# A new table of thresholds for the order planner of a gated two-branch attention kernel

## The chip, the cores and the metric

The kernel runs on one core of a Trainium2 chip. Its engines are named as the profile names them: PE (TensorE, matrix products; PEld is its weight load), DVE (VectorE), ACT (ScalarE), POOL (GpSimd) and SP (SyncE, which issues the DMAs). The metric is the time of one execution on the device in microseconds. The kernel before was timed three times: 816.85, 817.59 and 822.19 us, median 817.59.

## What is computed

For 2,048 tokens of width 640 and 32 heads of width 20: branch A is full softmax attention, branch B attends to 8 positions, its own and those 2, 4 ... 14 before it, and a gate per token mixes the two.

```python
x = A_x
g = _sigmoid((x * gate_w).sum(-1, keepdims=True))
a = _A_ref(x, A_wqkv, A_wo)      # full attention
b = _B_ref(x, B_wqkv, B_wo)      # window of 8, dilation 2
return g * a + (1 - g) * b

# _A_ref
scores = jnp.einsum("bhqd,bhkd->bhqk", q, k) * scale
p = _softmax(scores, axis=-1)
o = jnp.einsum("bhqk,bhkd->bhqd", p, v)
...
# _B_ref: W, dil = 8, 2; idx = pos - off, masked where negative
logits = jnp.einsum("bhsd,bhswd->bhsw", q, kg) * scale
attn = _softmax(logits, axis=-1)
o = jnp.einsum("bhsw,bhswd->bhsd", attn, vg)
```

## The kernel before

**Blocks and tiles.** The scores of branch A are cut into blocks of 128 keys x 512 queries of one head: 32 heads x 4 query chunks x 16 key blocks = 2,048 blocks. Four heads and one query chunk make a group of 64 blocks, and there are 32 groups. `next_tile` puts two or three blocks of one group together to a tile; `qk` (L1556 to L1587) issues their score matmuls (L1569) into one of two score buffers in PSUM, and `exp` (L1589) has ACT take the exponential of the whole tile in one instruction (L1592), two-wide (128 x 1024) or three-wide (128 x 1536). The third 512 columns of a score buffer are a bank which is also lent to other work, so a tile is three-wide only when that bank is free.

**Blocks on DVE.** Where a tile is two-wide, its third bank can hold a block that "rides": `wanted` decides whether DVE takes it. DVE then computes the exponential as an integer: it adds an offset and converts to 16 bits (L1582), so that the bits read as bf16 are 2 to a power, piecewise linear. Four such blocks make a quad in a buffer `uD`. To smooth the error, the product with the values is taken four times: DVE shifts the bits (L811, three times for a quad), and PE multiplies each version with the values times a weight. The weighted values are made by POOL (L804, `vS`). A block on ACT costs PE one product with the values (L1633), a block on DVE four.

**Other work.** Generators produce the projections of queries, keys and values (L573 is the helper that issues their matmuls, and DVE copies them out of PSUM), the gate, the whole of branch B (products on DVE at L882 and L980, two exponentials per 256 tokens on ACT), the normalization of a finished group, and the output projection (`gen_fold`). They run in the gaps. POOL copies the weights of branch B into padded form in 15 pieces (L828). Where PE would have too little to do, `filler` (L1654) issues products whose result is not used.

**What sets the order.** The kernel carries a planner. `_Sched.task` keeps, for each engine, the time until which it is taken, and every operation has a written duration. The main loop walks over the tiles: it issues the score matmuls and the exponential of tile s, then products with the values, then lets the generators spend PE's time up to a limit: the planned end of the exponential before, plus SLACK. The result is one fixed list of instructions for each engine; on the chip each engine runs its list in order, and semaphores hold it where an operand is not there. No decision is taken on the chip.

**The table.** `PLAN` (L50) holds, for certain tiles s, 21 thresholds which hold from that tile on (they are set in the main loop, after L1742). The ones that the text needs:

- SLACK: how far past the planned end of the exponential before other PE work may reach, for two-wide and three-wide tiles
- DWAIT, DIDLE, DIDLE2, DTIME: how free DVE must be, and how much of a group must still lie ahead, for DVE to take a block
- XTOL, XPRIO, XLATE: whether a tile takes the third bank, or other work gets it
- DVE_AHEAD, DAHEAD: how far DVE may be planned ahead of PE
- FILL: the share of PE's time below which filler products are issued
- MAXQ: how many quads of DVE may be open

Of the kernel before, what the change touches and what calls it, by code (L numbers as in the profile page):

```python
# [50 lines left out]
    0: ((0.36, 0.65), 0.4, 2.5, 2.5, 0.49, -1.3, -0.1, 11.8, 7.0, 7.2, 0.47, 0.47, 5.39, 4.0, -0.05, 0.69, 2, 0, 0.5, 4.0, 3.0),  # L51
    10: ((0.37, 0.65), 0.4, 1.0, 6.6, 0.71, -1.3, -0.19, 11.8, 7.0, 7.2, 0.47, 0.43, 5.39, 4.0, -0.05, 0.69, 2, 0, 0.48, 4.0, 3.0),
    20: ((0.43, 0.65), 0.4, 6.6, 2.5, 0.45, -1.3, -0.1, 11.8, 7.0, 8.27, 0.47, 0.47, 5.39, 4.0, -0.18, 0.69, 2, 0, 0.5, 4.0, 1.0),
    40: ((0.36, 0.65), 0.4, 2.5, 2.5, 0.49, -1.3, -0.1, 11.8, 7.0, 7.2, 0.47, 0.47, 5.39, 4.0, -0.13, 0.69, 2, 0, 0.5, 4.0, 3.0),
    50: ((0.36, 0.65), 0.4, 2.5, 1.0, 0.49, -1.08, -0.36, 11.8, 7.0, 7.2, 0.73, 0.66, 5.39, 4.95, -0.13, 0.69, 2, 0, 0.5, 4.0, 3.0),
    60: ((0.36, 0.65), 0.5, 2.5, 1.0, 0.49, -1.08, -0.36, 11.09, 1.0, 7.2, 0.73, 0.66, 5.75, 4.94, -0.13, 0.69, 2, 0, 0.5, 4.0, 3.0),
    70: ((0.36, 0.65), 0.5, 2.5, 1.0, 0.74, -1.08, -0.36, 11.09, 1.0, 7.2, 0.73, 0.66, 5.75, 4.94, -0.13, 0.69, 2, 0, 0.5, 4.0, 3.0),
    80: ((0.28, 0.65), 0.5, 2.5, 1.0, 0.74, -1.08, -0.68, 11.09, 1.0, 7.2, 0.73, 0.66, 5.75, 4.94, -0.13, 0.69, 2, 0, 0.5, 4.0, 3.0),
    100: ((0.43, 0.66), 0.4, 6.6, 2.5, 0.45, -1.56, 0.05, 12.31, 7.0, 8.27, 0.47, 0.47, 5.39, 4.0, -0.18, 0.69, 2, 0, 0.5, 4.0, 1.0),
    110: ((0.43, 0.66), 0.4, 6.6, 2.5, 0.45, -1.56, -0.19, 12.31, 7.0, 8.27, 0.47, 0.47, 5.39, 4.0, -0.18, 0.69, 2, 0, 0.62, 4.0, 1.0),  # L60
    120: ((0.43, 0.66), 0.37, 6.6, 2.5, 0.45, -1.56, -0.19, 12.31, 7.0, 8.27, 0.47, 0.47, 5.39, 4.0, -0.18, 0.69, 2, -3, 0.62, 4.0, 1.0),
    130: ((0.43, 0.65), 0.4, 6.6, 2.5, 0.45, -1.36, -0.42, 11.8, 7.0, 8.27, 0.47, 0.47, 5.39, 4.69, -0.18, 0.62, 2, 0, 0.5, 4.0, 3.0),
    140: ((0.39, 0.65), 0.4, 6.6, 2.5, 0.36, -1.36, -0.42, 11.8, 7.0, 8.27, 0.48, 0.47, 5.39, 4.69, -0.18, 0.62, 2, 0, 0.5, 4.0, 3.0),
    160: ((0.3, 0.64), 0.32, 2.5, 2.5, 0.49, -1.3, -0.1, 11.8, 7.0, 7.2, 0.52, 0.47, 3.94, 4.0, 0.0, 0.74, 2, 0.0, 0.5, 4.0, 3.0),
    180: ((0.3, 0.64), 0.32, 2.5, 2.5, 0.49, -1.42, -0.1, 13.5, 6.7, 7.2, 0.52, 0.47, 3.94, 4.0, 0.0, 0.58, 2, 0.0, 0.5, 4.0, 3.0),
    190: ((0.39, 0.65), 0.4, 6.6, 5.5, 0.36, -1.36, -0.42, 11.8, 6.7, 8.27, 0.48, 0.47, 6.32, 5.13, -0.18, 0.61, 2, -3, 0.5, 4.0, 3.0),
    200: ((0.3, 0.61), 0.32, 2.5, 2.5, 0.56, -1.3, -0.1, 11.8, 7.0, 7.2, 0.46, 0.47, 4.84, 4.53, 0.0, 0.74, 2, -3, 0.5, 4.0, 3.0),
    210: ((0.34, 0.61), 0.32, 2.5, 5.5, 0.76, -1.34, -0.1, 13.49, 7.0, 7.2, 0.4, 0.47, 4.84, 4.53, 0.0, 0.74, 2, -3, 0.73, 4.0, 3.0),
    220: ((0.34, 0.61), 0.32, 2.5, 5.5, 0.76, -1.27, -0.1, 13.49, 7.0, 8.55, 0.4, 0.47, 3.4, 4.53, 0.0, 0.74, 2, -3, 0.73, 4.0, 3.0),
    230: ((0.34, 0.61), 0.32, 6.6, 5.5, 0.76, -1.27, -0.1, 13.49, 7.0, 8.55, 0.35, 0.47, 3.4, 4.53, 0.0, 0.74, 2, -3, 0.73, 4.0, 3.0),  # L70
    240: ((0.28, 0.61), 0.32, 6.6, 5.5, 0.76, -1.02, -0.1, 13.49, 7.0, 8.55, 0.35, 0.55, 3.4, 4.53, 0.04, 0.69, 2, 1, 0.73, 4.0, 3.0),
    250: ((0.28, 0.66), 0.32, 6.6, 5.5, 0.76, -1.02, 0.4, 13.7, 7.0, 8.55, 0.46, 0.55, 4.08, 4.53, 0.04, 0.7, 2, 1, 0.73, 4.0, 3.0),
    260: ((0.31, 0.64), 0.32, 2.5, 2.5, 0.49, -1.42, -0.1, 13.5, 6.2, 7.2, 0.52, 0.47, 3.98, 4.0, 0.18, 0.58, 2, 0.0, 0.5, 4.0, 3.0),
    270: ((0.28, 0.69), 0.5, 2.5, 1.0, 0.74, -1.08, -0.7, 12.02, 1.0, 7.2, 0.72, 0.64, 5.75, 4.94, -0.13, 0.69, 2, 0, 0.55, 4.0, 3.0),
    280: ((0.26, 0.69), 0.5, 5.5, 1.0, 0.74, -1.08, -0.7, 14.18, 1.0, 5.68, 0.72, 0.64, 5.75, 4.94, -0.13, 0.52, 2, 0, 0.55, 4.0, 3.0),
    290: ((0.26, 0.69), 0.5, 5.5, 1.0, 0.74, -1.08, -0.7, 14.18, 1.0, 5.68, 0.79, 0.64, 5.75, 4.94, -0.13, 0.52, 2, 0, 0.55, 4.0, 3.0),
    300: ((0.26, 0.75), 0.5, 5.5, 1.0, 0.74, -1.08, -0.7, 14.18, 1.0, 5.68, 0.79, 0.64, 4.85, 4.78, -0.13, 0.52, 2, -1.5, 0.55, 4.0, 4.0),
    310: ((0.28, 0.69), 0.5, 2.5, 1.0, 0.74, -1.08, -0.58, 11.09, 6.7, 7.2, 0.72, 0.64, 5.75, 4.94, -0.13, 0.69, 2, 0, 0.5, 4.0, 3.0),
    320: ((0.31, 0.69), 0.5, 2.5, 1.0, 0.74, -1.08, -0.58, 11.09, 6.7, 7.2, 0.9, 0.64, 5.75, 4.94, -0.13, 0.69, 2, 0, 0.27, 4.0, 3.0),
    330: ((0.43, 0.75), 0.4, 1.0, 2.5, 0.49, -1.3, -0.29, 11.8, 7.0, 10.3, 0.47, 0.47, 5.39, 4.0, -0.18, 0.69, 1, 0, 0.34, 4.0, 3.0),  # L80
    340: ((0.36, 0.65), 0.35, 2.5, 6.6, 0.49, -1.3, -0.1, 11.8, 1.0, 7.2, 0.47, 0.47, 5.39, 4.0, -0.18, 0.69, 2, 0, 0.5, 4.0, 3.0),
    350: ((0.33, 0.65), 0.23, 2.5, 6.6, 0.49, -1.3, -0.1, 11.8, 1.0, 7.2, 0.47, 0.47, 5.39, 4.0, -0.18, 0.69, 2, 0, 0.5, 4.0, 3.0),
    360: ((0.36, 0.65), 0.35, 2.5, 6.6, 0.49, -1.3, -0.1, 10.56, 1.0, 7.2, 0.37, 0.47, 5.39, 4.0, -0.18, 0.69, 2, 0, 0.56, 4.0, 3.0),
    370: ((0.36, 0.58), 0.35, 2.5, 6.6, 0.49, -1.3, -0.1, 10.56, 1.0, 7.2, 0.23, 0.47, 6.86, 3.97, -0.18, 0.64, 2, 0, 0.21, 4.0, 3.0),
    380: ((0.43, 0.65), 0.4, 6.6, 5.5, 0.45, -1.36, -0.42, 12.51, 7.0, 8.27, 0.62, 0.47, 5.16, 4.69, -0.2, 0.62, 2, 1, 0.5, 4.0, 3.0),
    390: ((0.43, 0.45), 0.4, 6.6, 5.5, 0.45, -1.36, -0.42, 12.51, 7.0, 8.27, 0.62, 0.28, 5.16, 4.69, -0.25, 0.62, 2, -3, 0.5, 4.0, 4.0),
    410: ((0.43, 0.75), 0.4, 1.0, 2.5, 0.49, -1.35, -0.29, 11.8, 1.0, 10.3, 0.47, 0.47, 5.39, 4.54, -0.18, 0.76, 1, 0, 0.34, 4.0, 4.0),
    420: ((0.31, 0.6), 0.5, 2.5, 1.0, 0.49, -1.6, -0.36, 11.09, 1.0, 7.2, 0.73, 0.66, 5.75, 4.94, -0.13, 0.69, 2, 0, 0.5, 4.0, 3.0),
    430: ((0.38, 0.6), 0.5, 2.5, 1.0, 0.49, -1.6, -0.36, 10.37, 1.0, 7.87, 0.73, 0.66, 5.75, 4.94, -0.11, 0.69, 2, -3, 0.42, 4.0, 3.0),
    440: ((0.28, 0.69), 0.58, 2.5, 1.0, 0.74, -1.08, -0.7, 11.09, 1.0, 7.2, 0.72, 0.64, 5.75, 4.94, -0.13, 0.69, 2, -3, 0.46, 4.0, 3.0),  # L90
    450: ((0.26, 0.75), 0.3, 5.5, 1.0, 0.74, -1.08, -0.7, 14.18, 1.0, 5.68, 0.79, 0.64, 4.85, 4.78, -0.13, 0.52, 2, -1.5, 0.55, 4.0, 4.0),
    460: ((0.36, 0.65), 0.4, 6.6, 2.5, 0.49, -1.59, -0.1, 13.22, 7.0, 7.2, 0.31, 0.46, 5.39, 4.0, -0.31, 0.69, 2, 0, 0.5, 4.0, 2.0),
    470: ((0.33, 0.69), 0.61, 5.5, 1.0, 0.74, -1.08, -0.7, 12.02, 1.0, 7.2, 0.59, 0.64, 6.24, 5.94, -0.13, 0.69, 2, 0, 0.55, 4.0, 4.0),
    480: ((0.28, 0.69), 0.5, 2.5, 1.0, 0.74, -1.08, -0.7, 11.09, 1.0, 7.2, 0.73, 0.64, 5.75, 4.94, -0.13, 0.69, 2, 0, 0.5, 4.0, 3.0),
    490: ((0.53, 0.65), 0.4, 2.5, 2.5, 0.8, -1.3, -0.1, 11.8, 1.0, 7.2, 0.53, 0.5, 5.39, 4.0, -0.05, 0.61, 2, -1.5, 0.5, 4.0, 4.0),
    500: ((0.46, 0.65), 0.4, 2.5, 2.5, 0.8, -1.3, -0.1, 11.8, 1.0, 7.2, 0.53, 0.5, 5.39, 4.0, 0.04, 0.61, 2, -1.5, 0.5, 4.0, 3.0),
    510: ((0.47, 0.65), 0.24, 2.5, 6.6, 0.84, -1.3, -0.01, 11.8, 1.0, 7.2, 0.53, 0.66, 5.01, 4.0, 0.04, 0.61, 2, -1.5, 0.5, 4.0, 3.0),
    520: ((0.47, 0.65), 0.38, 2.5, 6.6, 0.67, -1.3, -0.01, 11.8, 1.0, 7.2, 0.53, 0.66, 5.01, 4.0, 0.04, 0.61, 2, -1.5, 0.5, 4.0, 3.0),
    530: ((0.47, 0.72), 0.38, 2.5, 6.6, 0.83, -1.3, -0.01, 11.8, 1.0, 7.2, 0.53, 0.66, 5.01, 4.0, 0.04, 0.61, 2, -1.5, 0.5, 4.0, 3.0),
    540: ((0.28, 0.69), 0.5, 5.5, 1.0, 0.74, -1.08, -1.0, 12.02, 1.0, 7.2, 0.72, 0.64, 5.75, 4.53, -0.13, 0.69, 2, 0, 0.55, 4.0, 2.0),  # L100
# [1727 lines left out]
```

## Time and profile before

| what | value |
|---|---|
| median of three runs | 817.59 us |
| profiled execution | 816.9 us, its span (first to last instruction) 815.2 us |
| granted PE clock, mean | 1.000 |
| instructions | 28,683 |
| tiles of the exponential (L1592) | 726: 480 two-wide, 245 three-wide, one of 512 |
| blocks on DVE (L1582) | 352, with 264 shifts (L811) |
| first tile starts, last tile starts | 19.35 us, 806.03 us |
| DMA | 35.71 MB in 61,412 packets, mean 44 GB/s |

A row of a group of instructions reads: line, engine, operation, output <- input by the program's names, shapes, count | busy time in us, mean ns of one | idle time of the engine just before them, and what released it. A row of the timeline reads: start in us, length in us, engine, line, operation, output <- input, shapes, count; in brackets the idle time before it and what ended that. Consecutive instructions of an engine overlap in the record, so that the mean of one can be longer than the distance between two starts.

How the engines share the span, by stretches: before the first tile, to the end of the copies of weights, the long middle, and the end.

```profile
core 0: us, PE busy (x) PEld busy (x) DVE busy (x) ACT busy (x) POOL busy (x), PEclk, DMA share, GB/s
0.00:19.35 19.35, 16.21 (x131) 9.99 (x137) 12.89 (x33) 8.76 (x12) 10.10 (x19) 1.00 0.94 303
19.35:170.00 150.65, 140.28 (x2070) 48.38 (x2067) 109.88 (x211) 145.40 (x134) 36.47 (x39) 1.00 0.18 44
170.00:806.00 636.00, 594.79 (x9800) 215.19 (x9792) 570.86 (x990) 633.98 (x613) 97.13 (x144) 1.00 0.15 35
806.00:815.20 9.20, 4.86 (x96) 1.89 (x88) 4.31 (x8) 1.81 (x4) 0.00 (x0) 1.00 0.21 73
```

ACT is busy from the first tile to the last; PE's busy time includes pipelined matmuls, so it is not PE at its peak.

### The profile page before, as it was taken

What the parts mean: (1) busy time and instruction counts of PE and PEld (TensorE: products, weight loads), DVE (VectorE), ACT (ScalarE), POOL (GpSimd) and SP (SyncE); (2) the same over time, 40 slices, a digit from 0 to 9 for tenths busy, and PEclk for the clock granted to TensorE, in tenths of its full rate; (3) what the DMA queues carried; (4) which work ended last, traced back from release to release, by engine and by line L of the source; (5) the groups of instructions that cost most, each with busy time, mean ns of one, the idle gap of its engine ahead of it and who ended that gap; (6) DMA issues with size and microseconds to landing.
All of it is one profiled execution on the core that took longest, in us unless ns stands there. A gap on an engine that the chain in (4) does not pass through costs nothing.

```text
span 815.2 us, 28683 instructions
## 1 busy us (share of the span) xinstructions
PE 756.1 (93%) x12077; PEld 275.4 (34%) x12079; DVE 697.9 (86%) x1241; ACT 789.9 (97%) x760; POOL 143.7 (18%) x201
## 2 busy tenths in 40 slices
PE   8999999998989999999999999998999999988997
PEld 5332223334433323333322433333333333432322
DVE  6675798678898998989998897899999989888994
ACT  4999999999999999999999999999999999999996
POOL 5030141231111211211101111120220120111210
PEclk9999999999999999999999999999999999999999
DMA  9103222002202101102101210310310022102001
GB/s 308 43 17 63 47 46 68 21 2 47 65 22 67 45 11 22 49 20 66 30 16 44 48 37 20 68 44 7 74 27 19 24 53 44 34 21 64 6 6 35
DMA packets 61412, 35.71 MB, mean 44 GB/s; under 512 B 27220, under 2 KB 60084, under 8 KB 61284
## 3 DMA queue, kind: packets, MB, share of 16 engines
q1 hardware_dynamic: 60996, 33.54, 16.7%
q8 instruction: 96, 1.57, 0.8%
q10 hardware_dynamic: 288, 0.33, 0.1%
q14 instruction: 32, 0.26, 0.1%
HBM read 11.94 MB, written 2.62 MB: 18 GB/s over the span
## 4 chain that ended last, share of the span: by engine, by line
ACT 42%; PE 26%; issue 19%; DVE 11%; DMA 1%; POOL 0%; ACTq 0%; SPq 0%; DVEq 0%
ACT ebuf L1592 42%; PE score L1569 9%; PE obank L1633 7%; PE side L573 6%; DVE uD L811 3%; DVE uD L1582 3%; PE score L573 2%; DVE stage L882 2%; DVE stage L980 1%; DMA oTd<-in_A_x_dram 1%; DVE qkvB L866 1%; PE side L898 1%; ACT eB L929 0%; PE score L1087 0%; PE score L1263 0%
## 5 line engine op out<-in xcount | busy, mean ns | idle before, releaser
L1592 ACT ACTIVATE ebuf<-score 128x1024 bf16<-128x1024 f32 (+1 forms) x726 | 777.6, 1232 | 7.8 <-PE score L1569 6.5
L1569 PE MATMUL score<-qT,kT 32*128 32x512 bf16 x2048 | 292.7, 384 | 44.9 <-ACT ebuf L1592 34.4
L1582 DVE TENSOR_SCALAR uD<-score 128x512 int16<-128x512 f32 x352 | 235.3, 681 | 26.3 <-PE score L1569 24.8
L811 DVE TENSOR_SCALAR uD<-uD 128x2048 int16<-128x2048 int16 x264 | 184.6, 717 | 13.2 <-PE obank L1633 12.4
L1633 PE MATMUL obank<-ebuf,vA 128*21 128x512 bf16 x1696 | 167.7, 386 | 2.4 <-DVE uD L811 1.4
L1569 PEld LDWEIGHTS score<-qT,kT 32*128 32x128 bf16 x2048 | 71.2, 91 | 289.7 <-ACT ebuf L1592 221.4
L804 POOL TENSOR_TENSOR vS<-vA,vw 128x252 bf16<-128x252 bf16 x88 | 65.2, 746 | 288.8 <-PE obank L1633 265.0
L573 PE MATMUL side<-xT,kvw 128*32 128x256 bf16 (+2 forms) x2430 | 98.3, 284 | 1.4 <-DVE qkvB L866 1.0
L1633 PE MATMUL obank<-uD,vS 128*21 128x512 bf16 x1056 | 92.8, 380 | 0.0
L1633 PEld LDWEIGHTS obank<-ebuf,vA 128*21 128x21 bf16 x1696 | 41.6, 88 | 102.7 <-issue 77.2
L573 PEld LDWEIGHTS side<-xT,kvw 128*32 128x32 bf16 (+1 forms) x2430 | 58.6, 96 | 33.5 <-issue 14.9
L780 POOL TENSOR_TENSOR rcp<-rcp,gA 128x16 f32<-128x16 f32 x31 | 8.5, 273 | 319.2 <-DVE rcp L778 319.2
L980 DVE TENSOR_TENSOR stage<-stage,eB 128x1280 bf16<-128x1280 bf16 x64 | 51.8, 829 | 0.0
L882 DVE TENSOR_TENSOR stage<-qkvB 128x1280 bf16<-128x1280 bf16 x64 | 51.2, 837 | 0.2
L866 DVE CAST qkvB<-side 128x512 bf16<-128x512 f32 (+1 forms) x66 | 38.5, 592 | 4.4 <-PE side L573 4.4
L786 POOL TENSOR_TENSOR oN<-oTt,rcp 128x512 bf16<-128x512 f32 x31 | 32.6, 1051 | 2.4
L1633 PE MATMUL obank<-uD,vA 128*21 128x512 bf16 x352 | 31.4, 379 | 0.0
L774 DVE STREAM_TRANSPOSE oTt<-obank 128x512 f32<-128x512 f32 x32 | 22.7, 710 | 8.5 <-PE obank L1633 8.1
L1633 PEld LDWEIGHTS obank<-uD,vS 128*21 128x21 bf16 x1056 | 25.1, 90 | 10.0 <-issue 3.4
L573 PE MATMUL side<-woBp,oB 128*32 128x128 bf16 (+1 forms) x540 | 27.0, 298 | 0.0
L573 PE MATMUL side<-woA_d,oTd 128*32 128x128 bf16 (+2 forms) x492 | 25.8, 300 | 0.0
L828 POOL COPY kvw<-stage 128x640 bf16<-128x640 bf16 x15 | 20.9, 1397 | 5.1 <-PE side L573 3.3
(189 smaller groups left out, 524.6 us busy)
## 6 DMA issues: line engine op xcount, KB each, us to landing
stage<-qkvB SPq DMA_DIRECT2D x128, 82.5 KB
WqP<-in_A_wqkv_dram SPq DMA_DIRECT2D x16, 160.0 KB
stage<-in_B_wqkv_dram SPq DMA_DIRECT2D x1, 2400.0 KB
oTd<-oN SPq DMA_DIRECT2D x108, 20.0 KB
qT<-dst SPq DMA_DIRECT2D x104, 20.0 KB
out_dram<-outsb SPq DMA_DIRECT2D x12, 160.0 KB
kvw<-in_A_wqkv_dram SPq DMA_DIRECT2D x2, 800.0 KB
qT<-qbnd SPq DMA_DIRECT2D x72, 1.0 KB
```

What stands on the lines that cost most here:

```text
L573: ins = e.matmul(o[j:k, :], l(j) if callable(l) else l[:, j:k], r, start=(first and i == 0), stop=(last and i == n - 1), skip_group_check= ...
L774: T("dve", 0.623, lambda e: e.transpose(oTt[:, :], obank[:, :]), reads=["obank"], writes=["oTt"])
L786: T(en, c2, lambda e: e.tensor_tensor(oo, ii, ib, ALU.mult), reads=["rcp", "oTt"], writes=["oN0"])
L804: T("pool", 0.7, lambda e: e.tensor_tensor(vS[:, d % NVS, :, :], _ap(vA, (kb * NQ + q) * 4 * DV, [[0, K - 1], [1, 4 * DV]]), _ap(vw, 0, [[ ...
L811: T("dve", 0.066 + 0.1334 * n, lambda e, k=k: e.tensor_scalar(uD[u][:, 0:512 * n].bitcast(I16), uD[u][:, 0:512 * n].bitcast(I16), SHIFTS[k ...
L866: t = TB(dvc(n * TOK), lambda e, o=o, i=i: e.tensor_copy(o, i), reads=[("side", b)], writes=[key])
L882: TB(dvc(CN * TOK, 2), lambda e, w=w, ks=ks: e.tensor_tensor(prodB(w), qB[:, :, :], ks, ALU.mult), reads=["qB", "kB"], writes=[("prod", w) ...
L980: TB(dvc(CN * TOK, 2), lambda e, o=o, vs=vs, ee=ee: e.tensor_tensor(o, vs, ee, ALU.mult), reads=["eB", ("prod", k)], writes=[("prod", k + ...
L1569: ins = e.matmul(o, kT[32 * j:32 * j + 32, q, kb * P:(kb + 1) * P], qT[g % NQT][32 * j:32 * j + 32, :], start=True, stop=True)
L1582: t = T("dve", 0.6, lambda e: e.tensor_scalar(uD[d % NU][:, 512 * i:512 * (i + 1)].bitcast(I16), side[x], UOFF, 0.0, op0=ALU.add, op1=ALU. ...
L1592: exps[s] = T("act", actc(512 * n), lambda e: e.activation(ebuf[s % NE][:, 0:512 * n], score[s % 2][:, 0:512 * n], ACTF.Exp, scale=LN2 / S ...
L1633: ins = e.matmul(obank[32 * j:32 * j + DV, :], v, src, start=(kb == 0), stop=(last and k >= len(lst) - 4), skip_group_check=True)
```

## The change

Every number of the table is replaced, and nothing else: the planner, the operations and their written durations stay as they are. The table has 66 entries instead of 61, most of them ten tiles apart in both. It comes from a search that keeps four partial layouts, tries more candidates and looks further ahead. The five added entries move all later lines down by five (L1592 is L1597 in the changed kernel).

```diff
 PLAN = {
-    0: ((0.36, 0.65), 0.4, 2.5, 2.5, 0.49, -1.3, -0.1, 11.8, 7.0, 7.2, 0.47, 0.47, 5.39, 4.0, -0.05, 0.69, 2, 0, 0.5, 4.0, 3.0),
-    10: ((0.37, 0.65), 0.4, 1.0, 6.6, 0.71, -1.3, -0.19, 11.8, 7.0, 7.2, 0.47, 0.43, 5.39, 4.0, -0.05, 0.69, 2, 0, 0.48, 4.0, 3.0),
...
-    700: ((0.28, 0.71), 0.47, 2.5, 1.0, 0.74, -0.52, -0.7, 12.02, 6.7, 7.2, 0.58, 0.64, 4.93, 4.94, -0.17, 0.69, 2, 0, 0.55, 4.0, 3.0),
-    710: ((0.28, 0.69), 0.5, 2.5, 1.0, 1.07, -1.08, -0.7, 12.02, 1.0, 7.2, 0.72, 0.42, 6.71, 4.94, -0.13, 0.69, 2, -3, 0.37, 4.0, 3.0),
+    0: ((0.28, 0.64), 0.32, 2.5, 2.5, 0.64, -1.3, -0.1, 11.8, 7.0, 7.2, 0.4, 0.7, 4.4, 4.0, 0.0, 0.75, 2, 0.0, 0.49, 4.0, 3.0),
+    10: ((0.28, 0.64), 0.32, 2.5, 2.5, 0.64, -1.3, 0.16, 11.8, 7.0, 7.2, 0.4, 0.7, 4.4, 4.0, 0.0, 0.61, 2, 0.0, 0.49, 4.0, 3.0),
...
+    700: ((0.28, 0.55), 0.26, 5.5, 2.5, 0.48, -1.26, -0.68, 15.76, 5.5, 9.18, 0.2, 0.61, 4.23, 2.97, -0.12, 0.8, 2, -3, 0.31, 4.0, 4.0),
+    710: ((0.28, 0.74), 0.32, 2.5, 2.5, 0.64, -1.3, -0.1, 11.8, 7.0, 7.2, 0.28, 0.68, 4.4, 4.0, 0.0, 0.75, 2, -3, 0.29, 4.0, 3.0),
 }
```

The order of the numbers in an entry is (SLACK, XTOL, XPRIO, XLATE, DWAIT, DIDLE, DIDLE2, DTIME, DLOW, DLATE, DVE_AHEAD, DAHEAD, BOOST, XBOOST, RFILL, FILL, HOLD, BOFF, BNEED, PVMIN, MAXQ). Averaged over the tiles, SLACK of a two-wide tile goes from 0.34 to 0.28 and stays at 0.66 for a three-wide one, DIDLE2 goes from -0.39 to 0.23, DVE_AHEAD from 0.60 to 0.38, DAHEAD from 0.55 to 0.71, FILL stays at 0.67.

## The prediction

> **What bounds the kernel now.** I read the page's busy times first, then the idle time and the waits of the busiest engine, then its timeline close up, then the two other engines that feed it. The page's busy times:
>
> ```profile
> PE 756.1 (93%) x12077; PEld 275.4 (34%) x12079; DVE 697.9 (86%) x1241; ACT 789.9 (97%) x760; POOL 143.7 (18%) x201
> ```
>
> ACT is busy 97% of the span, and all but 2% of that is one line, the exponential (L1592). The groups of instructions with shapes kept apart:
>
> ```profile
> L1592 ACT ACTIVATE ebuf<-score 128x1024 bf16<-128x1024 f32 x480 | 467.1, 1084 | 4.6 <-PE score L1569 3.4
> L1592 ACT ACTIVATE ebuf<-score 128x1536 bf16<-128x1536 f32 x245 | 349.8, 1522 | 3.2 <-PE score L1569 3.1
> ...
> L1582 DVE TENSOR_SCALAR uD<-score 128x512 int16<-128x512 f32 x352 | 235.3, 681 | 26.3 <-PE score L1569 24.8
> L811 DVE TENSOR_SCALAR uD<-uD 128x2048 int16<-128x2048 int16 x264 | 184.6, 717 | 13.2 <-PE obank L1633 12.4
> ```
>
> The means of 1084 and 1522 ns overlap their successors, so they are not what a tile costs. Two unbroken stretches of ACT's timeline give that (start, length, count):
>
> ```profile
> 46.10 9.64 ACT L1592 ACTIVATE ebuf<-score 128x1536 bf16<-128x1536 f32 x7
> ```
> ```profile
> 124.61 8.38 ACT L1592 ACTIVATE ebuf<-score 128x1024 bf16<-128x1024 f32 x9
> ```
>
> The last of the seven lasts 1.651 us, so six spacings take 9.64 - 1.65 = 7.99, 1.331 each; the last of the nine lasts 1.142, so eight take 7.24, 0.905 each. The start times of the single instructions say the same: the commonest spacing is 1,331 ns after a three-wide tile and 904 after a two-wide one. 512 elements more cost 427 ns, so a tile has about 50 ns of its own.
>
> From the first tile's start (19.35) to the last one's (806.03) are 786.7 us. Of these 480 x 0.904 + 245 x 1.331 = 760.0 are tiles, 5.1 the other activations among them (8 x 0.477, 8 x 0.104, 4 x 0.12), and the rest, 21.4 us, is ACT waiting. The rows above show only 3.4 + 3.1 of it as idle, since a start up to 0.2 us late hides in the overlap. So: 19.35 start + 760.0 tiles + 5.1 + 21.4 stalls + 9.2 end = 815.1.
>
> Where a stall comes from, in the timeline of one stretch on all engines:
>
> ```profile
> 116.14 3.10 POOL L828 COPY kvw<-stage 128x640 bf16<-128x640 bf16 x2
> 116.20 1.85 DVE L811 TENSOR_SCALAR uD<-uD 128x2048 int16<-128x2048 int16 x1
> ...
> 118.10 0.40 PE L1633 MATMUL obank<-ebuf,vA 128*21 128x512 bf16 x4 [0.66 <-DVE uD L811]
> 118.32 0.39 PE L1633 MATMUL obank<-uD,vS 128*21 128x512 bf16 x4
> ...
> 118.79 0.39 PE L1569 MATMUL score<-qT,kT 32*128 32x512 bf16 x3
> ...
> 119.23 2.02 ACT L1592 ACTIVATE ebuf<-score 128x1024 bf16<-128x1024 f32 x2 [0.71 <-PE score L1569]
> ```
>
> PE works strictly in list order: it waited for a slow DVE shift, the score group queued behind, and ACT ran dry.
>
> **The change, part by part.** Only numbers of the table change, so no row of the page is removed as such; what changes is the order that comes out. The two instruction lists differ in these counts.
>
> ACT: 480 two-wide and 245 three-wide tiles become 543 and 199 (and the one of 512 stays): 1,696 blocks become 1,684, since DVE takes 364 instead of 352, in 743 tiles instead of 726. Cost: 543 x 0.904 + 199 x 1.331 = 755.7 against 760.0, **-4.3 us**, all on the path. (12 blocks x 0.427 = -5.1, 17 more tiles x 0.05 = +0.85.)
>
> DVE: +12 of L1582 at 235.3/352 = 0.67 and +9 of L811 at 184.6/264 = 0.70 are +14.3 us of busy time: 712 in 811, 88%. Cover: DVE's idle time shrinks from 117 to 99 us. In the record's start times both run 0.60 apart when back to back, so the real load is about 656 us. At nothing; if the cover were gone, at most those 14.3.
>
> PE: 12 blocks with four weighted products instead of one are +36 matmuls, +9 rounds of four at 0.22 (118.10 to 118.32) = +2.0; filler groups (L1654) fall from 141 to 130, -2.4. Nothing. POOL: +3 of L804 x 0.746 = 2.2 us, under 671 us idle. DMA issues: 726 in both lists, same kinds. Nothing.
>
> Start and end: the lists agree up to the fifth score group, with it the 1.97 us that ACT loses ahead of its second tile (40 projection matmuls in front of the score group). Behind the last score group stand three rounds of PE work instead of four, and the last DVE shift has three tiles of time. At nothing; 0.2 us either way.
>
> Stalls: the rest, 19.5 us without that second tile. No row shows them for an order not run, so I sort the stalls of before by two things that a list shows: the width of the tile that ACT is working on, and the PE work that stands between its score group and the next. After a three-wide tile (244) the mean stall is 6 ns. After a two-wide tile: 17 ns with under 0.6 us of PE work (341 cases), 75 with 0.6 to 0.8 (110), 134 with more (29). The new list has 198, 415, 110 and 18 of these: 1.1 + 7.2 + 8.3 + 2.4 = 19.0, **-0.5 us**. More boundaries of two-wide tiles, fewer overfull ones. Bounds: by width alone (38 ns after a two-wide, 6 after a three-wide) it would be 21.6, +2.1; sorted also by whether the last two slots of PE work come within 0.25 us of ACT's two tiles, 17.1, -2.4. I take the middle one, which rests on the fuller classes. Their scatter, if cases are independent, is 2.2 us on the sum, so 2.8 either way holds 8 in 10.
>
> POOL's copies (L828, 15) and L804 can stretch L811: 22 of 264 shifts lasted over 745 ns (median 685), 8.6 us together. Two of those under a copy (1.85 us at 116.20, 1.62 at 161.72) made ACT lose 1.4 and 0.7; a third (1.47 at 167.46) nothing. Whether the new order has more such hits the list can't tell: zero to seven, -2 to +5 us; I take as many as now.
>
> The Trainium skill's "GPSIMD Engine Reference" (1. Specifications) says that GpSimd shares its SBUF interfaces with VectorE and contends with DVE instructions that use two ports or two SBUF inputs. The trace agrees at 116.20. Charged in full for the three added L804 that is 2.2 us of DVE time, an estimate, under 99 us of idle; the sum stays.
>
> Sum: span 815.2 - 4.3 - 0.5 = 810.4. The profiled execution took 816.9, 1.7 more than its span: 812.1. The median of the runs (817.59) is 0.7 above it: **812.8 us**, 0.6% less.
>
> **Rivals.**
> *A: the stalls go too.* The new order may also avoid the hits of POOL on DVE and fill fewer slots that PE then can't clear. For: slots with over 0.8 us of PE work after a two-wide tile fall from 29 to 18, over 1.25 us after a three-wide from 22 to 8. Against: 63 more two-wide tiles, each with only 0.9 us of cover. Price: -4.3 - 2.4 - 2.1 (both hits gone) and half of the 1.58 us before the tile at 161.1, -9.6: 808.0.
> *B: slower, POOL's copies meet DVE's shifts.* Place: the 15 copies of 1.34 us in the first quarter. Each hit holds a shift 0.9 to 1.2 us, PE behind it, and costs ACT (1.4 + 0.7)/2 = 1.05. It decides from five more hits on (4.8 us); with six, 819. For: two hits in this trace; a third without harm. Against: only 28 shifts lie before 170 us, where the copies end, and three were hit; the new list has 24 up to its 128th tile, the same stretch.
> *C: slower, PE's clock falls.* Fewer fillers, 130 rounds for 141. The trace shows the slow clock: the nine first matmuls (column: min/median/max)
>
> ```profile
> L474 PE MATMUL obank<-qabs x9: 379/631/631, 1.2 to 6.5; 128*128 128x512 bf16 x9
> ```
>
> start 427 ns apart and last 631 ns; from 6.5 us on no matmul lasts over 420. With rounds twice as long, PE's load of 0.76 of ACT's time becomes 1.5, half a us lost for each; 13 us (to 1% slower) need 26 us of slow clock. Against: over any eight tiles PE's work is at least 0.54 of ACT's in the new list, 0.53 in the old. About 826.
> The Trainium skill's "TensorE: Matmul & The Clock Gate" (What's actually happening) has the array fall to half clock after at least one idle window of about 3.4 us, which speaks against dropping fillers. In this trace the emptiest 3.41 us after 20 us is still 49% busy at full speed, so by that rule too nothing is lost here.
> *D: no gain.* The new boundaries stall like the old by width alone, and two more hits: -4.3 + 2.1 + 2.1: 817.5.
>
> **How the numbers follow.** Forecast 0.64 (809.4 to 816), A 0.19, B 0.10, C 0.02, D 0.05. 1% is 8.2 us, about what a measurement of this kernel can tell from no change: below 809.4 is faster, above 825.8 slower. Faster: A, 0.19. Slower: C and the far end of B, 0.04. Within: 0.77. Range: A reaches down to 806 (a quarter of it beyond), B is cut in its middle: 806 to 818.5 leaves out about 0.13.
>
> **What would show it.** ACT: 743 tiles, 543 and 199, spaced 904 and 1,331, busy about 786 us. Stalls between first and last tile near 21. DVE near 712 us busy. For A: stalls under 17; for B: shifts of 1.4 us and more under L828 between 46 and 170 us, each with a gap on ACT behind it; for C: matmuls of 600 ns after 20 us. Stalls above 26 would break the sum.

## The result, and the profile after

The changed kernel takes 811.3 us (median of six executions, 809.85 to 811.66). The kernel before, run on the same chip in turn, took 818.75 (six executions, 816.85 to 822.19). The ratio is 0.990, interval 0.988 to 0.993: about 7 us or 0.9% faster, just inside the 1% that the prediction called the same. The forecast was 812.8. A later set (below, "after again") gave 811.47 against 817.86, ratio 0.992 (0.991 to 0.994).

The profiled execution after took 811.51 us, its span 809.7, at a mean PE clock of 0.996. Its busy times:

```profile
PE 763.0 (94%) x12071; PEld 272.4 (34%) x12071; DVE 711.9 (88%) x1262; ACT 785.5 (97%) x777; POOL 151.8 (19%) x204
```

ACT at 785.5 and DVE at 711.9 are where the prediction put them (786 and 712). The groups with shapes kept apart, after:

```profile
L1597 ACT ACTIVATE ebuf<-score 128x1024 bf16<-128x1024 f32 x543 | 528.4, 1103 | 1.1 <-PE score L1574 0.6
...
L1597 ACT ACTIVATE ebuf<-score 128x1536 bf16<-128x1536 f32 x199 | 292.0, 1536 | 3.4 <-PE score L1574 3.3
L1587 DVE TENSOR_SCALAR uD<-score 128x512 int16<-128x512 f32 x364 | 243.2, 680 | 20.5 <-PE score L1574 18.9
L816 DVE TENSOR_SCALAR uD<-uD 128x2048 int16<-128x2048 int16 x273 | 192.2, 723 | 9.8 <-PE obank L1638 9.1
```

The counts are those of the lists. ACT's idle time just before two-wide tiles fell from 4.6 to 1.1 us: that belongs to a larger fall which these rows show only in part, because a start up to 0.2 us late hides in the overlap. Worked out from the start times of all tiles, in the way of the prediction:

| | before | after | forecast |
|---|---|---|---|
| first tile starts | 19.35 | 21.15 | 19.35 |
| tiles and other activations | 765.3 | 761.1 | 760.8 |
| stalls between first and last tile | 21.3 | 18.05 | 20.9 |
| from the last tile's start to the end | 9.3 | 9.4 | 9.2 |
| span | 815.2 | 809.7 | 810.4 |

By these start times the last tile before begins at 805.96 us rather than at 806.03, hence 21.3 us of stalls and 9.3 at the end. So the tiles gave their 4.2 us, the stalls 3.2 instead of 0.5, and 1.8 were lost at the start. The start is in the windows after, to be set against the four windows before (columns: busy us and count of PE, weight loads, DVE, ACT, POOL, then granted PE clock, DMA share, GB/s):

```profile
0.00:21.15 21.15, 16.84 (x133) 10.46 (x137) 12.90 (x33) 8.74 (x12) 10.10 (x19) 0.92 0.88 278
21.15:170.00 148.85, 142.13 (x2065) 47.26 (x2059) 108.95 (x212) 146.40 (x139) 38.02 (x39) 1.00 0.18 45
170.00:800.30 630.30, 599.48 (x9801) 212.92 (x9793) 585.77 (x1011) 628.68 (x625) 103.69 (x147) 1.00 0.15 36
800.30:809.70 9.40, 4.58 (x92) 1.78 (x84) 4.29 (x8) 1.69 (x4) 0.00 (x0) 0.85 0.21 71
```

PE's clock is 0.92 over the start, where it was 1.00 before. (The column counts the time ahead of the first clock record, 6.25 us in before and 4.78 in after, as full.) PE's timeline there shows why:

```profile
4.61 1.37 PE L1268 MATMUL score<-ident,oTd 128*128 128x128 bf16 x20
5.82 0.38 PE L479 MATMUL obank<-qabs 128*128 128x512 bf16 x1
8.81 2.32 PE L1268 MATMUL score<-ident,oTd 128*128 128x128 bf16 x20 [2.61 <-DMA oTd<-in_A_x_dram]
10.91 1.38 PE L1294 MATMUL side<-xT,kvw 128*128 128x512 bf16 x4
```

Twenty transposes take 1.37 us before the wait for x and 2.32 after it: the clock had opened at 4.78 us, PE stood idle for 2.6 us, and the clock record reads half from 8.20 to 11.61 us. The two lists agree up to the fifth score group, so this needs a test before it is put down to the change.

The stalls: before had two episodes in which POOL's copies stretched a shift of DVE (1.4 us of stalls behind the shift at 116.20, and 0.7 at 164.5 behind the one at 161.72), and one single stall of 1.58 us ahead of the tile at 161.1. That one, in before's timeline on all engines:

```profile
158.95 0.58 PE L573 MATMUL score<-kvw,xT 128*32 128x320 bf16 x12
...
159.59 0.49 DVE L742 CAST vA<-score 128x320 bf16<-128x320 f32 x1 [0.24 <-PE score L573]
...
160.13 0.40 PE L1633 MATMUL obank<-ebuf,vA 128*21 128x512 bf16 x4 [0.60 <-DVE vA L742]
...
160.67 0.39 PE L1569 MATMUL score<-qT,kT 32*128 32x512 bf16 x3
...
161.11 2.85 ACT L1592 ACTIVATE ebuf<-score 128x1024 bf16<-128x1024 f32 x3 [1.42 <-PE score L1569]
```

Products with the values waited for the values, which PE had only just projected and DVE was copying out; the score group stood behind them in PE's list. After has one episode. Its timeline on all engines:

```profile
121.92 4.51 POOL L833 COPY kvw<-stage 128x640 bf16<-128x640 bf16 x3
...
123.59 1.61 DVE L816 TENSOR_SCALAR uD<-uD 128x2048 int16<-128x2048 int16 x1
123.73 0.53 PEld L578 LDWEIGHTS side<-kvw,xT 128*32 128x32 bf16 x20 [1.05 <-DVE vA L747]
123.73 0.86 PE L578 MATMUL side<-kvw,xT 128*32 128x320 bf16 x20 [0.75 <-DVE vA L747]
...
124.52 0.61 PE L1574 MATMUL score<-qT,kT 32*128 32x512 bf16 x6
...
124.96 1.45 ACT L1597 ACTIVATE ebuf<-score 128x1536 bf16<-128x1536 f32 x1 [0.48 <-PE score L1574]
```

It costs 0.73 us. Two more long shifts (0.91 us at 65.08 and 0.94 at 167.98) cost nothing; with the copies cut (e11, below) both are gone.

### The profile page after: what moved, and what is told of

The parts are those of the page before. It is cut to its first block, busy times and chain, and to the rows that moved or that the text cites. A ratio compares the mean times of both kernels' runs of the same rounds, so it can differ in the third digit from the quotient of the medians.

```text
span 809.7 us, 28705 instructions
## 1 busy us (share of the span) xinstructions
PE 763.0 (94%) x12071; PEld 272.4 (34%) x12071; DVE 711.9 (88%) x1262; ACT 785.5 (97%) x777; POOL 151.8 (19%) x204
## 4 chain that ended last, share of the span: by engine, by line
ACT 40%; PE 31%; issue 16%; DVE 11%; DMA 1%; ACTq 0%; SPq 0%; DVEq 0%
ACT ebuf L1597 39%; PE score L1574 11%; PE obank L1638 9%; PE side L578 7%; DVE uD L1587 3%; DVE uD L816 3%; PE score L578 2%; DVE stage L887 1%; DVE stage L985 1%; DMA oTd<-in_A_x_dram 1%; DVE qkvB L871 1%; PE obank L1659 1%; PE score L1268 1%; ACT eB L934 1%; PE score L1092 0%
## 5 line engine op out<-in xcount | busy, mean ns | idle before, releaser
L1597 ACT ACTIVATE ebuf<-score 128x1024 bf16<-128x1024 f32 (+1 forms) x743 | 773.1, 1219 | 4.6 <-PE score L1574 3.9
L1574 PE MATMUL score<-qT,kT 32*128 32x512 bf16 x2048 | 299.2, 384 | 32.2 <-ACT ebuf L1597 22.4
L1587 DVE TENSOR_SCALAR uD<-score 128x512 int16<-128x512 f32 x364 | 243.2, 680 | 20.5 <-PE score L1574 18.9
L816 DVE TENSOR_SCALAR uD<-uD 128x2048 int16<-128x2048 int16 x273 | 192.2, 723 | 9.8 <-PE obank L1638 9.1
L809 POOL TENSOR_TENSOR vS<-vA,vw 128x252 bf16<-128x252 bf16 x91 | 73.1, 811 | 249.9 <-PE obank L1638 249.8
L578 PE MATMUL side<-xT,kvw 128*32 128x256 bf16 (+1 forms) x2100 | 85.8, 282 | 0.7 <-DVE qkvB L871 0.4
L578 PEld LDWEIGHTS side<-xT,kvw 128*32 128x32 bf16 x2100 | 50.0, 96 | 27.8 <-issue 13.9
L871 DVE CAST qkvB<-side 128x512 bf16<-128x512 f32 (+1 forms) x58 | 33.7, 590 | 2.4 <-PE side L578 2.3
L578 PE MATMUL score<-xT,kvw 128*32 128x256 bf16 (+2 forms) x660 | 34.9, 307 | 0.0
L1638 PEld LDWEIGHTS obank<-uD,vS 128*21 128x21 bf16 x1092 | 25.5, 90 | 10.4 <-issue 2.5
L578 PE MATMUL side<-kvw,xT 128*32 128x320 bf16 x520 | 23.9, 301 | 1.6 <-DVE vA L747 1.3
```

The source lines that it names most:

```text
L578: ins = e.matmul(o[j:k, :], l(j) if callable(l) else l[:, j:k], r, start=(first and i == 0), stop=(last and i == n - 1), skip_group_check= ...
L809: T("pool", 0.7, lambda e: e.tensor_tensor(vS[:, d % NVS, :, :], _ap(vA, (kb * NQ + q) * 4 * DV, [[0, K - 1], [1, 4 * DV]]), _ap(vw, 0, [[ ...
L816: T("dve", 0.066 + 0.1334 * n, lambda e, k=k: e.tensor_scalar(uD[u][:, 0:512 * n].bitcast(I16), uD[u][:, 0:512 * n].bitcast(I16), SHIFTS[k ...
L871: t = TB(dvc(n * TOK), lambda e, o=o, i=i: e.tensor_copy(o, i), reads=[("side", b)], writes=[key])
L1574: ins = e.matmul(o, kT[32 * j:32 * j + 32, q, kb * P:(kb + 1) * P], qT[g % NQT][32 * j:32 * j + 32, :], start=True, stop=True)
L1587: t = T("dve", 0.6, lambda e: e.tensor_scalar(uD[d % NU][:, 512 * i:512 * (i + 1)].bitcast(I16), side[x], UOFF, 0.0, op0=ALU.add, op1=ALU. ...
```

## The experiments

My theory at this point: ACT's tiles count one for one; the stalls fell by two episodes and one single stall; the late start belongs to one execution. Rivals: ACT isn't what sets the pace, and less work on it would come back as waits on PE; the hits of POOL cost nothing; the new list delays the start.

**e1: less work on ACT, same lists.** In after, from tile 60 on:

```diff
-            ebuf[s % NE][:, 0:512 * n], score[s % 2][:, 0:512 * n], ACTF.Exp, scale=LN2 / STEP),
+            ebuf[s % NE][:, 0:512 * n - (48 if s >= 60 else 0)], score[s % 2][:, 0:512 * n - (48 if s >= 60 else 0)],
+            ACTF.Exp, scale=LN2 / STEP),
```

> The changed kernel's list, with each exponential from the 60th tile on leaving out its last 48 columns (those keep older values), so 40 ns less ACT work in each of 683 tiles, 27.3 us together. Theory (ACT's tiles are the path, so a block less on ACT is worth its 427 ns): from the first tile's start to the last one's, 779.1 us now, at least 15 us go, and the stalls of 18.2 grow by at most 12. Rival (the hand-overs between PE, DVE and ACT in the list set the pace, and the gain came from a better order): less than 9 us go, since PE's and DVE's lists are the same, and the stalls grow by 18 or more.

Measured: 804.2 us, span 802.4. From first to last tile 774.06 us where after has 779.11: 5.05 of the 27.3 us came, and the stalls rose from 18.05 to 40.3. My theory fell and the rival held. How PE stands to ACT shows in the waits of PE's weight loads (total us, times, longest). After:

```profile
PEld score L1574 <- ACT ebuf L1597: 228.0, 545, 1.2
...
PEld score L1574 <- issue: 38.8, 134, 0.4
```

The trimmed kernel:

```profile
PEld score L1574 <- ACT ebuf L1597: 165.6, 394, 1.2
PEld score L1574 <- issue: 88.8, 282, 0.6
```

In 151 more cases PE does not wait for ACT to free a score buffer: it comes to the score group after ACT is done, from other work in its list. Among two-wide tiles with 0.6 to 0.68 us of PE work between score groups (105 in both) the mean stall went from 68 to 151 ns. I read this so: the planner fills the room beside a tile with PE work, and a shorter tile meets a PE list laid out for a longer one.

**e7 and e8: less work on PE, same lists.** In after (e7) and in the trimmed kernel (e8) each filler is cut from four matmuls to a short one:

```diff
-            for j in range(4):
-                ins = e.matmul(o[32 * j:32 * j + 32, :], w[:, 32 * j:32 * j + 32] if best else w[:, :], xT[:, 0, 0:512], start=bool(best),
-                               stop=bool(best), skip_group_check=True)
+            ins = e.matmul(o[0:32, 0:64], w[:, 0:32] if best else w[:, :], xT[:, 0, 0:64], start=bool(best),
+                           stop=bool(best), skip_group_check=True)
```

> After's lists, each filler (four matmuls of 512 columns that add zero, or that write a bank before it is used) cut to one of 64 columns: some 20 us less on PE in the same order. If the fillers sit only where PE would wait anyway, the run stays within 1 us of 811 with stalls of 17 to 19 us. If they delay the next score matmuls, stalls fall by 2 to 6 us. If they hold PE's clock up, matmuls of 600 ns appear after 25 us and the run is slower by 3 us or more.

> Both edits: every exp from tile 60 on 48 columns shorter (the last 48 columns of a tile keep an earlier tile's values) and the fillers cut short. If what held the trimmed run at 804 is the sheer length of PE's list, 20 us less of it gives back 8 to 20 us: 784 to 796. If it is the hand-overs (score banks freed by ACT and DVE, uD tiles from DVE), 802 to 804. If PE's clock falls, slower than 804 with matmuls of 600 ns.

Measured: e7 816.25 us, 5 slower than after; e8 810.8, 6.6 slower than e1. Of e7's 24.52 us of stalls 6.45 lie in three stretches in which matmuls of a doubled length appear (140 in all), where after loses 0.6; the other 18.07 are close to after's 18.05. So the fillers stand where PE would wait, and what they do in these runs, one execution each, is hold the clock. One of the stretches, e7:

```profile
157.00:164.00 7.00, 5.12 (x69) 1.59 (x57) 5.21 (x9) 7.00 (x9) 6.61 (x7) 1.00 0.05 13
164.00:171.00 7.00, 6.82 (x77) 2.36 (x73) 4.28 (x9) 5.22 (x5) 2.62 (x3) 0.51 0.01 2
```

and after in the same windows:

```profile
157.00:164.00 7.00, 5.85 (x83) 1.84 (x75) 5.22 (x11) 7.00 (x8) 5.69 (x6) 1.00 0.05 12
164.00:171.00 7.00, 6.61 (x104) 2.46 (x104) 6.11 (x12) 7.00 (x8) 4.32 (x5) 1.00 0.02 6
```

With 5.12 us of PE work in seven the clock fell to 0.51 in the next seven, and ACT lost 1.8 of them. In e8, 7.2 of 44.3 us of stalls are such stretches; the other 37.1 are 3.2 under e1's 40.3. So the length of the fillers is not what held e1; PE's other work was not shortened. That leaves this work and the order within the list; I did not isolate which hand-over.

**e5 and e6: other tables with shorter ACT lists.** e5 takes one column (DVE_AHEAD) of before's table from after's, at all entries; e6 takes before's entries from tile 240 on into after's table.

```diff
-    0: ((0.36, 0.65), 0.4, 2.5, 2.5, 0.49, -1.3, -0.1, 11.8, 7.0, 7.2, 0.47, 0.47, 5.39, 4.0, -0.05, 0.69, 2, 0, 0.5, 4.0, 3.0),
+    0: ((0.36, 0.65), 0.4, 2.5, 2.5, 0.49, -1.3, -0.1, 11.8, 7.0, 7.2, 0.4, 0.47, 5.39, 4.0, -0.05, 0.69, 2, 0, 0.5, 4.0, 3.0),
...
```
```diff
-    240: ((0.28, 0.67), 0.35, 2.5, 2.5, 0.86, -1.3, 0.8, 14.42, 6.7, 7.2, 0.39, 0.83, 4.4, 3.53, 0.1, 0.61, 2, -1.5, 0.31, 4.0, 3.0),
+    240: ((0.28, 0.61), 0.32, 6.6, 5.5, 0.76, -1.02, -0.1, 13.49, 7.0, 8.55, 0.35, 0.55, 3.4, 4.53, 0.04, 0.69, 2, 1, 0.73, 4.0, 3.0),
...
```

> Before's table with one column, DVE_AHEAD, taken from after's: 487 two-wide and 226 three-wide tiles, 1,652 blocks on ACT (741.1 us at 904 and 1,331 ns), 396 rides. Theory that ACT's tiles count one for one: 19.35 + 741.1 + 5.1 + 21 + 9.3 = span 795.9, run 797.6. Rival from the trimmed run, in which 27.3 us less on ACT brought 5.05: PE's hand-overs and DVE (about 44 more rides than before at 1.2 us each, so some 750 us busy) take most of it back, stalls 30 us or more, run 805 to 811; slower than after (811.3) if DVE itself falls behind.

> After's table up to tile 240 and before's from there: 469 two-wide, 243 three-wide and 1 one-wide tile, 1,668 blocks (747.9 us), about 380 rides. One for one: 19.35 + 747.9 + 5.1 + 21 + 9.3 = span 802.7, run 804.4. Rival, 18 per cent as in the trimmed run: 811.3 minus 0.18 x 12.2 = 809 or later, with stalls near 28 us.

Measured: 1,048.3 us (ratio to before 1.280, 1.277 to 1.284) and 982.7 (1.201, 1.199 to 1.204). Both theories were far off. ACT's work is as short as the lists said (745.0 and 752.7 us), but the stalls are 271 and 196 us, and PE's mean clock in the two profiles is 0.907 and 0.934. Apart from the fillers, the choice of banks and the blocks that moved from ACT to DVE, both lists hold the operations of before, but the output that they compute is wrong: in these orders some value is overwritten or read at the wrong time, and which one was not traced. They say something about time alone. ACT's largest waits in e5:

```profile
ACT ebuf L1602 <- PE score L1579: 125.1, 37, 28.8
ACT eB L939 <- PE side L935: 107.8, 3, 41.6
```

Single waits of 29 and 42 us. In the chain of waits of e5 from 255 to 310 us, the engines work one after another on branch B: shifts and products on DVE, the transfers that SP issues, matmuls, the exponential L939 and again. A few lines of it (start, length, what):

```profile
255.46 0.60 DVE qkvB L876
256.05 2.21 DVE stage L892 x3
...
276.00 2.19 DMA stage<-qkvB
278.22 3.15 DVE stage L990 x5
...
300.43 1.29 PE side L908 x16
...
304.49 0.61 ACT eB L939
```

The eight exponentials L939 start at 217, 262, 304, 441, 476, 718, 758 and 974 us, in bunches, where those of before come 56 to 98 us apart. I read this as work put off until something needed it, with little else left to run beside it; the groups of filler matmuls rose from 141 to 314. That ACT's list was shorter because other work had been pushed behind it is argued, not shown. A count of tiles is therefore worth something only with a list whose other work comes in time. In after it does: its longest stall is the 1.97 us ahead of the second tile, which before has too.

**e2, e3, e10, e11: the hits of POOL's copies.** Each of the 15 copies is cut to 32 columns, in before (e2, then e10 in more executions) and in after (e3, e11); the one added line clears what is no longer written:

```diff
-                o = _ap(kvw, (m * CN + c) * D, [[P, CN], [32, 4], [1, 32]])
-                i = _ap(stage, c * 3 * D + m * D, [[1, CN], [CN, 4], [DH, 32]])
+                o = _ap(kvw, (m * CN + c) * D, [[1, 32]])
+                i = _ap(stage, c * 3 * D + m * D, [[DH, 32]])
...
+    T("pool", 0.0, lambda e: e.memset(kvw[:, WKP_OFF + D:3 * CN * D].bitcast(FP32), 0.0), writes=["kvwz"])
```

> The kernel before, with POOL's 15 copies (L828) cut to 32 of 640 columns (branch B is then computed with other weights), the lists being the same otherwise but for one early memset on POOL. Theory (POOL's copies hold DVE's shifts, PE's list waits behind them): no shift before 170 us lasts over 1.2 us, the stalls at 117 to 122 us (1.4) and at 164.5 (0.7) go, all stalls 21.4 to about 19.3; the 1.6 at 161 stays, as a projection forced in front of the products made it. Rival (the order makes these stalls anyway): 21 or more.

> The same cut in the changed kernel (branch B with other weights). Theory: only one hit cost ACT there (0.7 us at 125, behind the shift of 1.61 at 123.6), so the stalls go from 18.2 to about 17.5, and the two kernels then differ in stalls by 1.8 instead of 3.2. Rival (the order makes it): 18 or more.

> Before with POOL's weight copies cut to 32 columns (the rest of the rearranged weights is left out), timed over several executions: theory that the hits on DVE's shifts cost before the 2.3 us of its two episodes: executions of full clock go from 816.0 to 817.1 us to 813.5 to 815. If the hits were hidden anyway: 816 to 817.

> The same cut in after: its one costly hit is worth 0.7 us, so 808.5 to 810 where after itself gives 809.5 to 811.5. Against the cut kernel of before that leaves 4.5 to 5.5 us, which is the fall of ACT's tiles (4.3) and little else; if the new table saves more than tiles and hits, the two cut kernels stand further apart, by 6 us or more.

Measured:

| kernel | median us (executions) | stalls us | first to last tile us |
|---|---|---|---|
| before | 817.86 (16) | 21.3 | 786.6 |
| before, copies cut (e10) | 815.86 (11) | 19.3 | 784.6 |
| after (e9, below) | 811.47 (6) | 17.9 | 779.0 |
| after, copies cut (e11) | 809.36 (4) | 17.4 | 778.5 |

Medians are from one set on one chip; stalls and windows are from the profiled executions, that of before from the first profile. In e2 and e10 no shift ahead of 170 us lasts over 0.9 us, as the theory said, and the hits cost before 2.0 us in its stalls and 2.0 in its time (ratio 0.997, 0.996 to 0.998). In after the cut takes 0.5 us from the tiles' window; the rest of the 2.1 us between the two medians lies outside it (e11's profiled execution began its tiles 0.66 earlier and ended 0.97 sooner behind the last tile). e2 and e3, one execution each, gave 818.6 and 808.71. e3's stalls were 17.3. e2's were 23.1, of which 4.3 belong to something else, told below; the other 18.8 stand beside e10's 19.3.

The two cut kernels stand 6.5 us apart by their medians and 6.13 by their windows, more than the 4.5 to 5.5 that I expected. Of the 6.13, 4.2 are tiles and 1.9 stalls, and e10 still has the 1.58 us single stall (at 159.2 there), which no copy causes. What is left is 0.3.

**e9: after again.**

> The changed kernel as it is, beside the three others on one chip. Theory: the start of 21.15 in its profiled execution was that execution's own (its edit is not in the start), so that most executions begin their tiles at 18.9 to 19.5, the fastest spans are 807.5 to 808.5, and an execution with a later start has a lower mean clock (0.996 against 1.000). Rival: the new list itself delays the start by 1.8 us; then the first tile stands at 21 again.

Measured: 811.47 us (810.12 to 812.15). The first tile of the profiled execution stands at 19.57, so the list does not delay the start, and the rival falls. My own expectation held for the start and the fastest span (808.3), but not for the clock: it was 0.996 here too, because the clock fell in another place, in the output projection at the end:

```profile
798.00:804.00 6.00, 5.69 (x97) 2.31 (x93) 3.01 (x6) 1.89 (x4) 0.00 (x0) 0.85 0.01 3
```

Sixteen matmuls there last 631 to 634 ns, and the end takes 10.4 us instead of 9.4.

**e4 and e12: more warm-up between the two parts of x.**

```diff
-    for i in range(1):
-        T("pe", 0.215, warm_up, reads=[("qabs", 0)], writes=["obank"])
+    for i in range(10):
+        T("pe", 0.215 / 10, warm_up, reads=[("qabs", 0)], writes=["obank"])
```

> The changed kernel with ten warm-up matmuls instead of one between the first and the second turning of x, the lists being the same otherwise. Theory (in the profiled execution PE's clock fell back in the 3 us in which PE waited for the second part of x): the matmuls after 8 us last as in the kernel before (128x512 at 379 ns, none over 420 after 7 us), the first tile starts at 19.4 to 19.8 instead of 21.15, span 808 instead of 809.7. Rival (the DMA of x alone made the start late): the first tile starts near 21.

> After with ten matmuls of warm-up instead of one between the two parts of the first transposes. Theory: they keep PE at full clock over the wait for x, so that no execution starts its tiles after 20 us; the median falls by 0.5 to 1 us against after, to 809.5 to 810.5, and the spread narrows. Rival: the clock in the start goes by something else, and median and spread stay those of after.

Measured: e4 810.46 (one execution), e12 810.38 (five, 809.51 to 810.59). PE's start in e12, the windows around the wait:

```profile
5.00:9.00 4.00, 4.00 (x33) 2.66 (x31) 1.32 (x7) 1.02 (x1) 0.00 (x0) 1.00 0.98 304
9.00:12.00 3.00, 3.00 (x41) 2.23 (x39) 1.65 (x2) 1.08 (x2) 2.70 (x5) 1.00 1.10 347
```

No gap and no slow matmul. The first tile starts at 19.90 and 19.92, later than in most executions (18.9 to 19.6), probably since the ten matmuls stand in front of the second transposes, and earlier than in its first profile (21.15). The spread is 1.1 us against 2.0, the median 1.1 lower. All five executions have a mean clock of 0.998 to 1.000, where nine of the twelve of after have 0.994 to 0.997; that fits the theory. The two profiles do not show the gain, though: the first tile of e12 stands 0.35 us later than that of e9, first to last tile takes 779.3 us for 779.0, and what e9 loses is at its end. Against before the ratio is 0.991 (0.989 to 0.992), beside 0.992 (0.991 to 0.994) for after: it is the fastest version here that computes everything, but the intervals overlap.

## Why the prediction came out as it did

- **ACT's tiles, -4.3: right.** 765.3 to 761.1, at the same 904 and 1,331 ns per tile. What e1 and e5 add is that this was not owed to ACT's being busy 97%: time taken from its tiles alone comes back to less than a fifth, and a shorter list may stall. That it counted in full here because the list was planned anew as a whole, with PE work that grew no heavier beside its tiles, is argued, not shown. Nor is it shown which of the 21 thresholds brought the new order.
- **Stalls, -0.5: right in mechanism for the ordinary ones, mis-sized as a sum; -3.2 measured.** This is the step that failed. By class the forecast was 1.1 (three-wide), 7.2, 8.3 and 2.4 us (two-wide, by rising PE work); measured were 2.2, 5.2, 7.5 and 1.4, in all 16.3 for 19.0. The class means of before contained its three single events (1.4 + 0.7 + 1.58 us), and multiplying them by the new counts foretold three such events again. Without the events before has 15.8 us of ordinary stalls, and after without its one (0.73) 15.5. Rival A (chance 0.19) named the same events; it lacked only the one that after has of its own, and took 2.4 off the ordinary stalls besides, of which 0.3 came.
- **POOL on DVE, "as many as now": a near miss.** Shifts over 745 ns rose from 22 to 32 and their excess from 8.6 to 11.0 us, but long shifts are no measure of lost time: what ACT lost went from about 2.1 to 0.7. Rival B had the price right: e10 shows 2.0 us for two harmful hits, 1.0 each, where it took 1.05. It needed five more, and one fewer came.
- **Start and end at nothing: right for the list, wrong for the execution profiled.** The 1.8 us of late start and the 0.2 at the end are in that profile; e9 has the first tile at 19.57.
- **DVE, PE: right.** DVE +14.0 us busy, hidden; PE's time was not the limit (763.0). POOL rose by 8.1 us rather than 2.2, since L809 lasts longer on average; it has hundreds of us of idle time.
- **Rival C: wrong in what it said of before.** I wrote that before's emptiest 3.41 us are 49% busy at full speed and that nothing is lost there. By the estimate of the last section they are about 29% busy, and in e2, whose PE list is before's, the clock did fall. The price that I took, half a us lost for each us of slow clock, came close: e2 lost 4.3 us in 10.2, e7 6.45 in 17.1. That the new list has fewer fillers did no harm: in no profiled execution of its list with the fillers whole was a matmul slow between 13 us and the last tile.
- **From span to median.** 0.7 us were added for the median of before's three runs; its later sets have medians of 818.75, 817.11 and 817.86, so before lies 0.2 to 1.9 us above its profiled 816.9. The medians of after, 811.3 and 811.5, lie near its first profiled execution (811.51), which had the late start. That 812.8 came within 1.5 us of this is partly luck: the forecast had 2.9 us too many stalls, and the late start of 1.8, which nothing in it foresaw, took most of that back.

## What to carry to other kernels

When a whole order is replanned, count the bounding engine's instructions and take their spacing from the trace; that term was right to 0.1 us. Sort the stalls into ordinary ones, which follow the classes, and single events with a cause of their own, which need not recur in another order (after has just one, of 0.73 us): carry over the first and price the second one by one. An engine at 97% is not shown to be the limit until its work alone is shortened, and a planner's list with less work on it is only better if everything else still arrives in time.

## What the runs showed of the hardware

**PE's clock falls after short gaps, and after stretches that are only lightly loaded.** The wait for x at the start lasted 1.2 to 1.9 us between two starts on PE in ten profiled executions (before, e1 to e3, e5 to e7, e9 to e11): none had a slow matmul after it, and their tiles began at 18.9 to 19.6 us. In after's first profile it lasted 2.99 and in e8 2.60: both had matmuls of over 420 ns between 10.9 and 12.5 us, and tiles from 21.15 and 21.59 on. The length of the wait is the DMA's and changes from one execution to the next.

The Trainium skill's "TensorE: Matmul & The Clock Gate" (What's actually happening) has the clock fall after at least one idle window of about 3.4 us that runs freely. The gaps here that sufficed were shorter, 2.60 and 2.99 us. The clock records agree with a window that runs freely: within each of the 14 profiled executions all changes of the clock lie on a grid of 3.413 us, 98 changes in all, to 0.002 us, and the first one stands at 4.78 to 7.12 us. They do not agree that the window has to be idle: in after the clock fell at 8.20 us, while PE still waited for x, and in the window before, 4.78 to 8.20, PE had been busy for 1.42 us.

In the middle of the kernel no idle time of that length was needed at all. e2 and e10 are one kernel; the same stretch in e2

```profile
495.00:502.00 7.00, 5.21 (x91) 1.76 (x91) 3.87 (x13) 7.00 (x9) 2.96 (x5) 0.90 0.17 37
502.00:511.00 9.00, 9.00 (x98) 2.77 (x90) 4.56 (x8) 5.93 (x7) 0.00 (x0) 0.51 0.09 20
```

and in e10:

```profile
495.00:502.00 7.00, 5.21 (x99) 1.82 (x91) 3.87 (x12) 7.00 (x9) 2.96 (x5) 1.00 0.17 36
502.00:511.00 9.00, 8.43 (x137) 3.00 (x129) 8.15 (x16) 9.00 (x11) 0.00 (x0) 1.00 0.09 22
```

PE is as busy up to 502 us in both, 5.21 of 7 us with no idle time over 0.96; in e2 the clock then stands at 0.51 for nine microseconds and ACT loses 4.3, in e10 nothing happens. The clock record of e2 reads half from 500.61 to 510.85, three windows of the grid.

In these runs the fall goes by how PE is loaded within one window of the grid. For an estimate I weigh each matmul with its columns at full speed (512 take 213 ns, half of the 427 between two starts at the beginning) and with its share of 128 x 128 in steps of 32. The 14 profiles hold 3,299 windows at full clock:

| load of the window | windows | clock fell at its end |
|---|---|---|
| under 34% | 36 | 36 |
| 34 to 38% | 25 | 13 |
| over 38% | 3,238 | 0 |

e2's window from 497.20 us held 35%; e10's from 497.10 held just over 38%, since a score group that begins 0.24 us ahead of the window in e2 (496.96) begins with it in e10 (497.10). So the same list can keep its clock in one execution and lose it in another, by where the grid lies: the emptiest 3.4 us of before's list after 20 us (29% at 499.8 us) and those of e7 (18% at 565 us) lie across the border of two windows which both hold over 38%, and neither cost the clock. The least in after is 35%, at 403 us.

The times of whole executions go with the mean clock. Of before's 28 in the sets of the experiments, ten at 1.000 have a median of 817.0 us and four at 0.994 and less one of 821.2. Of after's twelve, the three at 0.999 and 1.000 took 809.9 to 810.1 us, the nine at 0.994 to 0.997 took 810.8 to 812.2. Where the clock fell is known for the profiled executions alone.
